# Weight reloads into any freed slot, and token changes spread over ten products, in a fused attention and two-MLP kernel

## The chip, the cores and the metric

The kernel runs as one program on one core of a Trainium2 chip. The metric is the device time of one launch in microseconds (us). Five engines work side by side: TensorE (PE, with its weight loads listed apart as PEld), VectorE (DVE), ScalarE (ACT), GpSimd (POOL) and SyncE (SP), which issues all of this kernel's DMAs. Each engine takes its own instructions in the order in which they were written; semaphores hold an instruction until what it reads has been made and what it overwrites has been read.

## The reference

```python
# attention: 4 batches, 8 heads, 576 tokens, head size 64, with a relative-position bias
attn_out = softmax(q @ k.T / 8 + bias) @ v          # -> x, 2304 tokens x 512
# first MLP, 512 -> 2048 -> 512
h = x @ w_in
x = (h - tanh(h)) @ w_out
# second MLP, 512 -> 1536 -> 512, gated
gate = 1 / (1 + exp(-(x @ w_gate)))
val = x @ w_val
out = (gate * val) @ w_out
```

All of it is in float32. The kernel splits each factor of a matrix product into a rounded part ("high", dtype fp32r) and the rest ("low") and adds three products, high by high, high by low and low by high.

## The kernel before, in words

Attention runs first, then the first MLP in 48 steps, then the second MLP. The change touches only the second MLP.

**Products and slots.** The second MLP takes its 1536 hidden features as six blocks of 256 (`fp`) and its 2304 tokens as three parts of 768 (`tau`). `SEGS` orders the work as five segments, each one token part with a run of feature blocks; a block in a segment is a *pair*, and there are 18 pairs (3, 3, 6, 3 and 3). Gate and value are made by a seven-product scheme (like Strassen's): seven combinations of the weights meet seven combinations of the tokens. A pair therefore has 14 *slots*, seven products for the gate (slots 0 to 6) and seven for the value (7 to 13). `slot2` writes one slot: it issues pending weight reloads (`feed`), writes the product (L866, six matmuls of 128x384 into one of two PSUM banks, `sum0` and `sum1`), then one piece of the output product of the pair before (`down`, L882, three matmuls of 128x512; twelve of the 14 slots have one, slots 12 and 13 have none), and then `evacuate`, which takes the bank's result out of PSUM. The product of slot s needs the bank that was used in slot s - 2, so its result must have been taken out by then. Most results are taken out by VectorE with an addition or a product (L927, L933, L937, L941, one operand in PSUM); the first of each seven, and the third of the gate, by ScalarE (L924, L931).

**Changing the tokens.** Between two segments the seven token combinations must be made anew. `src_load` brings the source, `combine` makes sums and differences on VectorE (L786 to L792), and `x_make` makes one half (`kp` 0 or 1) of one combination: a copy to fp32r for the high part, and a subtraction for the low part (both have line L797). In the kernel before, `x_next` does this in the slots 7 to 13 of a segment's last pair, both halves of one combination in each slot, as each combination is used there for the last time; the copies are on ScalarE, the subtractions on GpSimd for half 0 and on VectorE for half 1. I call the seven slots C0 to C6, and the slots that follow in the next segment C7 (its slot 0), C8, and so on. There are four such change-overs. The third combination also needs `combine(kp, 3)` (L792) behind it.

**Weights.** The nine weight tiles of a pair (seven combinations and two for the output product, 512 KB each) lie in DRAM (`wsc`) and are loaded into a ring of 13 SBUF slots in a fixed rotation: load number k goes where load number k - 13 was, and is issued once that one has been used up. The tiles of the blocks 3 to 5 are made on the way, in the first half of the second MLP: `convert` lets VectorE (L545 to L549), ScalarE (L533, L556) and GpSimd (L554, L604) work at one item in seven slots and stores the results from three staging slots.

Of the kernel before, what the change touches and what calls it, by code (L numbers as in the profile page):

```python
# [7 lines left out]
F32 = mybir.dt.float32  # L8
# [427 lines left out]
PRODUCTS = (1, 6, 2, 7, 5, 4, 3)  # L436
GROUPS2 = len(PRODUCTS)
SLOTS2 = 2 * GROUPS2
PER_FP = GROUPS2 + 2
X_SLOTS, T_SLOTS, RING_SLOTS = tuple(range(14)), (14, 15), 13  # L440
STAGE1 = (0, 1, 2, 3)
X0_AT = N1 - 4
SEGS = ((0, 0, 3), (1, 0, 3), (2, 0, NFP), (0, 3, NFP), (1, 3, NFP))
PAIRS = [(g, tau, fp, fp - lo, hi - lo) for g, (tau, lo, hi) in enumerate(SEGS) for fp in range(lo, hi)]
X0_STEPS = (X0_AT + 1, X0_AT + 2, X0_AT + 3)
# [189 lines left out]
def mlps(tc, st, xr, x0, W, xs, x2s, y2s, out, consts):  # L635
# [3 lines left out]
    V, A, G, T = nc.vector, nc.scalar, nc.gpsimd, nc.tensor  # L639
# [142 lines left out]
    def combine(kp, k):  # L782
        a, b = sx[kp], sx[2 + kp]
        if k == 0:
            tt_[kp] = W.slot(T_SLOTS[kp], (128, 2, TB)).bitcast(F32)
            V.tensor_sub(src(5, kp), a[:, TB:TP], a[:, 0:TB])  # L786
        elif k == 1:
            V.tensor_sub(src(7, kp), b[:, TB:TP], a[:, TB:TP])
        elif k == 2:
            V.tensor_sub(src(6, kp), b[:, TB:TP], src(5, kp))  # L790
        else:
            V.tensor_sub(b[:, 0:TB], b[:, 0:TB], src(6, kp))  # L792

    def x_make(j, kp, low):
        x, w = src(j, kp), W.slot(X_SLOTS[2 * PRODUCTS.index(j) + kp], (128, 2, TB))
        xw[j, kp] = w
        return (lambda: A.copy(w[:, 0], x)), (lambda: low.tensor_sub(w[:, 1], x, w[:, 0].bitcast(F32)))  # L797

    X0 = {X0_AT + 1: ([(kp, k) for kp in range(2) for k in range(3)], [(j, kp) for j in (1, 2) for kp in range(2)]),
          X0_AT + 2: ([], [(6, 0), (6, 1), (7, 0), (7, 1), (5, 0)]),  # L800
# [1 line left out]
          N1: ([], [(4, 0), (4, 1)])}  # L802

    loads = [(u, i) for u in range(len(PAIRS)) for i in range(PER_FP)]
    ring, held, issued, spent = [], {}, [0], set()

    def feed():
        while issued[0] < len(loads):
            k = issued[0]
            u, i = loads[k]  # L810
            fp = PAIRS[u][2]
            if (fp, i) not in W.stored or k >= len(ring) and (k < RING_SLOTS or loads[k - RING_SLOTS] not in spent):
                return
            w = W.slot(ring[k % RING_SLOTS])
            nc.sync.dma_start(w.bitcast(F32).rearrange("p a c -> p (a c)"), W.wsc[fp][i])
            held[loads[k]] = w
            issued[0] += 1

    freed = {W.of[k, f]: LAST[1, f // NPR] + (3 if k == "o" else 1) for k in "io" for f in range(FA, NF1)}
# [2 lines left out]
    def convert():  # L822
        while W.made <= W.n:
            highs, lows, mixes, conv = W.step()
            for f in conv[:2]:
                f()
                yield
            for f in highs + lows:
                f()
            for f in conv[2:]:  # L830
                f()
                yield
            for f in mixes:
                f()
            yield
            W.scan()
            yield
            yield
    banks, sums, posts, downs, res = [], [], {}, [], {}

    def at(s, f):
# [14 lines left out]

    def product(s):
        u, m, j = mat(s)
        w = held[u, j]
        p = banks[s % 2]  # L860
        fresh = j in (0, 1, 4)
        for kp in range(2):
            x = xw[PRODUCTS[j], kp]
            for i, (a, c) in enumerate(P3):
                o = 256 * m + 128 * kp
                T.matmul(p, w[:, a, o:o + 128], x[:, c], start=(fresh and kp == 0 and i == 0),  # L866
                         stop=(kp == 1 and i == 2), skip_group_check=True)
        if m:
            spent.add((u, j))

    def down():
        if not downs:
            return
        u, f, t, d, last = downs.pop(0)
        g, tau, fp, at_, n = PAIRS[u]
        h, l = res[u, f, t]
        w = held[u, GROUPS2 + f]
        begin = at_ == 0 and f == t
        end = at_ == n - 1 and f != t
        c = slice(128 * d, 128 * d + 128)  # L880
        for i, (x, a) in enumerate(((h, 0), (h, 1), (l, 0))):
            T.matmul(sums[3 * t + d], x[:, c], w[:, a], start=(begin and i == 0), stop=(end and i == 2))  # L882
        if last:
            spent.add((u, GROUPS2 + f))
        if end:
            return lambda: leave(g, t, d)

# [77 lines left out]
    def slot2(s):  # L965
        u, m, j = mat(s)
        g, tau, fp, p, n = PAIRS[u]
        W.tick()
        feed()
        product(s)  # L970
        left = down()
        evacuate(s)
        if left:
            at(s + 1, left)
        for f in posts.pop(s, []):
            f()
        if g + 1 < len(SEGS):
            if p == n - 3 and m == 1 and j < 4:
                src_load(SEGS[g + 1][0], j)
            if p == n - 2 and j < 3:  # L980
                combine(m, j)
            if p == n - 1 and m == 1:
                x_next(j)
        if SEGS[g][1] and p == n - 1 and m == 0 and j < 6:
            bring(tau, j)
        return g + 1 < len(SEGS) and (p == n - 2 and j < 3 or p == n - 1 and m == 1 and j == 2)

    def x_next(j):
        k = PRODUCTS[j]
        for kp in range(2):  # L990
            for f in x_make(k, kp, (G, V)[kp]):
                f()
        if k == 2:
            for kp in range(2):
                combine(kp, 3)

    def due(n, stage):
        return [m for m in range(n - 4, n) if ok(m) and n - m == LAGS[stage]]
# [1 line left out]
    s = 0  # L1000
    for n in range(N1 + 3):
        if n < N1:
            W.tick()
        if n == 2:
            acc = st.enter_context(tc.tile_pool(name="ps_a", bufs=4, space=PSUM, side="right"))
        acts = second(n - 1) if ok(n - 1) else []
        acts[2:2] = [lambda m=m: fourth(m) for m in due(n, 1)]
        vecs = [f for m in due(n, 0) for f in third(m)]
        low, mixes, conv = [], [], []
        if 2 <= n < N1 and n not in X0_STEPS and not any(ends(m) and block(m)[2] for m in due(n - 1, 2)):  # L1010
            h, low, mixes, conv = W.step()
            acts += h
        if n in X0:
            conv = [lambda p=p: combine(*p) for p in X0[n][0]]
        for f in acts:
            f()
        zip_run(vecs, conv)
        if n in X0:
            for p in X0[n][1]:
                h, l = x_make(*p, G)  # L1020
                h()
                low.append(l)
        if n == N1:
            only1.close()
            ev = st.enter_context(tc.tile_pool(name="p3e", bufs=6))
            upst.close()
            one = st.enter_context(tc.tile_pool(name="ps_w", bufs=1, space=PSUM))
            banks = [one.tile([128, 512], F32, name=f"sum{i}")[:, 0:TB] for i in range(2)]
            W.raw2 = st.enter_context(tc.tile_pool(name="wr2", bufs=2))
            ob2 = st.enter_context(tc.tile_pool(name="p2o2", bufs=2))  # L1030
            W.stages = RING[RING_SLOTS:]
            W.lag = 4
        for _ in range({N1: 2, N1 + 1: 5}.get(n, 0)):
            slot2(s)
            s += 1
        for m in due(n - 1, 2):
            if ends(m):
                sixth(m)
        if ok(n):
            for _ in first(n):  # L1040
                if n < 2:
                    yield
        for m in due(n, 2):
            fifth(m)
        for l in low + mixes:
            l()
        if n < N1:
            W.scan()
        if ok(n) and ok(n + 1):
            for ahead in range(1, 5):  # L1050
                if ok(n + ahead) and block(n + ahead - 1) != block(n + ahead):
                    for f, lead in ((x_split, 3), (x_load, 4)):
                        for kt in range(4):
                            if lead - kt // 2 == ahead:
                                f(block(n + ahead), kt)
        if ok(n - 1) and block(n - 1)[2] == 1 and ends(n - 1):
            partial(n - 1)
        if n == X0_AT:
            for kt in range(4):
                src_load(0, kt)  # L1060
        if n >= X0_AT:
            ring += [i for i in RING if freed[i] == n or n == X0_AT and freed[i] < n]
            ring[RING_SLOTS:] = []
            feed()
        yield
    b = odd.tile([128, 2, 512], F32, name="up")
    sums = [b[:, i] for i in range(2)] + [acc.tile([128, 512], F32, name="acc") for _ in range(4)]
    conv = convert()
    while s < SLOTS2 * len(PAIRS):
        full = slot2(s)  # L1070
        if s == SLOTS2 // 2:
            for _ in range(2):
                W.load()
        if s > SLOTS2 // 2 and not full:
            next(conv, None)
        s += 1
        yield
# [124 lines left out]
```

## Time and profile before

| | us |
|---|---|
| median of 3 runs | 1169.89 (1168.03 to 1171.68) |
| the profiled execution | 1171.4 |
| its span, first to last instruction | 1169.6 |
| TensorE busy in the span | 1122.9 (96%) |
| VectorE busy | 829.3 (71%) |
| ScalarE busy | 672.6 (58%) |
| GpSimd busy | 667.9 (57%) |
| mean granted TensorE clock | 0.989 |

The span is what the trace covers; the execution's own time is 1.8 us more. The second MLP begins at about 723 us with single products between steps of the first MLP, has TensorE to itself from about 739 us, and ends the span. An engine's idle time is listed with what ended it, as "idle before, releaser".

### The profile page before, as it was taken

How to read it: one execution, taken by the hardware profiler on the slowest of the kernel's cores; microseconds unless marked ns; L12 is line 12 of the kernel's file. 1: busy time of each engine (PE TensorE's matmuls, PEld its weight loads, DVE VectorE, ACT ScalarE, POOL GpSimd, SP SyncE). 2: the span in 40 equal slices, each digit the busy share in tenths (PEclk: the TensorE clock that was granted, in tenths of full speed). 3: DMA queues.
4: the chain of work that ended last, by engine and by line, in shares of the span. 5: the costliest groups of instructions: out<-in, count | busy, mean ns of one | idle time of the engine just before them, and what ended most of it. 6: DMA issues, size and time to landing. Idle time of an engine off the chain costs nothing.

```text
span 1169.6 us, 19994 instructions
## 1 busy us (share of the span) xinstructions
PE 1122.9 (96%) x6968; PEld 978.5 (84%) x6968; DVE 829.3 (71%) x1443; ACT 672.6 (58%) x1341; POOL 667.9 (57%) x602
## 2 busy tenths in 40 slices
PE   5679999999999999999999999999989999999998
PEld 2246776677679999999999999998879999989987
DVE  8878888888659889898889887556566523533523
ACT  7877878787657676677766667234244222423321
POOL 1047777778635555496858667455676543523532
PEclk9889999999999999999999999999999999999999
DMA  6754636373213333355665667876987875685563
GB/s 202 258 177 129 195 112 199 121 210 108 86 48 103 105 107 114 127 195 182 213 207 176 214 238 266 292 274 243 353 313 286 310 294 210 247 295 219 220 255 138
DMA packets 107636, 235.09 MB, mean 201 GB/s; under 512 B 12688, under 2 KB 52880, under 8 KB 107536
## 3 DMA queue, kind: packets, MB, share of 16 engines
q1 hardware_dynamic: 107536, 233.82, 57.7%
q8 instruction: 56, 0.92, 0.3%
q14 instruction: 44, 0.36, 0.1%
HBM read 172.55 MB, written 61.22 MB: 200 GB/s over the span
## 4 chain that ended last, share of the span: by engine, by line
PE 86%; DMA 3%; ACT 3%; DVE 2%; issue 2%; POOL 2%; SPq 0%; DVEq 0%; ACTq 0%; POOLq 0%
PE sum L866 20%; PE acc L727 16%; PE up L663 16%; PE acc L882 8%; PE sc L227 6%; PE pv L319 6%; PE pt L269 6%; PE up L882 4%; DMA w<-wsc 2%; PE bt L75 1%; PE pv L316 1%; ACT e L86 1%; ACT y L62 1%; DMA bsc<-e 1%; POOL w L554 1%
## 5 line engine op out<-in xcount | busy, mean ns | idle before, releaser
L866 PE MATMUL sum<-w,w 128*128 128x384 f32 x1512 | 304.2, 340 | 10.4 <-DMA w<-wsc 3.3
L866 PEld LDWEIGHTS sum<-w,w 128*128 128x128 f32 x1512 | 270.2, 188 | 35.5 <-issue 5.8
L663 PE MATMUL up<-xt,w 128*128 128x384 f32 x1152 | 208.4, 335 | 0.3 <-DVE t L697 0.3
L663 PEld LDWEIGHTS up<-xt,w 128*128 128x128 f32 x1152 | 200.1, 188 | 2.9 <-issue 2.2
L727 PE MATMUL acc<-gh,w 128*128 128x384 f32 x768 | 195.5, 335 | 0.1
L259 POOL TENSOR_SCALAR n<-n,rec 128x576 f32<-128x576 f32 x144 | 120.8, 853 | 83.4 <-ACT n L248 41.1
L554 POOL TENSOR_TENSOR w<-wu,w 128x512 fp32r<-128x512 f32 x86 | 128.4, 1504 | 64.5 <-ACT w L556 64.5
L708 POOL TENSOR_TENSOR gl<-t,gh 128x384 fp32r<-128x384 f32 x96 | 103.8, 1103 | 91.2 <-issue 51.1
L727 PEld LDWEIGHTS acc<-gh,w 128*128 128x128 f32 x768 | 138.3, 188 | 1.2 <-DVE o L746 1.1
L727 PE MATMUL acc<-gl,w 128*128 128x384 f32 x384 | 128.3, 334 | 0.0
L241 DVE CUSTOM_DVE_ANT_0 n<-sc,bias 128x576 f32<-128x576 f32 x144 | 103.7, 753 | 29.7 <-PE sc L227 25.8
L916 POOL TENSOR_TENSOR gl<-e,gh 128x384 fp32r<-128x384 f32 x54 | 58.7, 1092 | 101.7 <-ACT gh L701 101.7
L248 ACT ACTIVATE n<-n,mn 128x576 f32<-128x576 f32 x144 | 111.4, 783 | 8.7 <-DVE mn L241 8.6
L701 ACT CAST gh<-t 128x384 fp32r<-128x384 f32 x114 | 57.7, 516 | 60.4 <-POOL t L952 59.3
L692 ACT ACTIVATE z<-z,c 128x768 f32<-128x768 f32 x48 | 45.2, 941 | 78.9 <-DVE up L691 78.8
L882 PE MATMUL acc<-w,gh 128*128 128x512 f32 x288 | 90.1, 393 | 0.0
L693 DVE TENSOR_TENSOR t<-up,t 128x768 f32<-128x768 f32 x48 | 46.0, 958 | 53.4 <-ACT t L680 52.7
L269 PE MATMUL pt<-ident,n 128*128 128x128 f32 x576 | 80.4, 281 | 1.4 <-ACT at L299 1.3
L654 POOL TENSOR_TENSOR xt<-xm,xt 128x384 fp32r<-128x384 f32 x48 | 49.3, 1047 | 53.9 <-ACT xt L653 50.5
L319 PE MATMUL pv<-at,vs 128*64 128x320 f32 (+1 forms) x512 | 79.3, 421 | 0.0
L941 DVE TENSOR_TENSOR e<-sum,e 128x384 f32<-128x384 f32 x70 | 38.8, 555 | 52.0 <-PE sum L866 52.0
L269 PEld LDWEIGHTS pt<-ident,n 128*128 128x128 f32 x576 | 63.5, 141 | 12.6 <-issue 11.4
(111 smaller groups left out, 2145.5 us busy)
## 6 DMA issues: line engine op xcount, KB each, us to landing
w<-wsc SPq DMA_DIRECT2D x162, 512.0 KB, 7.4
wsc<-w SPq DMA_DIRECT2D x54, 512.0 KB, 5.6
wraw<-in_wo SPq DMA_DIRECT2D x28, 512.0 KB, 4.4
bsc<-e SPq DMA_DIRECT2D x36, 295.5 KB, 3.1
xm<-xs SPq DMA_DIRECT2D x48, 192.0 KB, 3.2
x2s<-o SPq DMA_DIRECT2D x48, 192.0 KB, 3.7
wraw<-in_wi SPq DMA_DIRECT2D x16, 512.0 KB, 4.3
xt<-x2s SPq DMA_DIRECT2D x20, 384.0 KB, 6.8
```

The costliest lines, as they stand in the source:

```text
L227: T.matmul(sc[u, t][:, hf, 0:288], q[r, 128 * s:128 * s + 128], k[r, o:o + 288], start=(i == 0), stop=(i == 2))
L241: V.tensor_tensor_reduce(n.rearrange("p (a b) -> p a b", a=2), s[:, :, 0:288], bias[t].rearrange("p (a b) -> p a b", a=2), -0.125, 3.0e38, ...
L248: A.activation(n, n, AF.Exp, bias=m, scale=-1.0, accum_out=nsum[u, t // 4][:, t % 4:t % 4 + 1])
L259: G.tensor_scalar(n, n, nrec[u, t // 4][:, t % 4:t % 4 + 1], 1.0, ALU.mult, ALU.mult)
L269: T.transpose(pt[:, i], n[:, o:o + 128], ident)
L319: T.matmul(p[0][64 * a:64 * a + 64, 0:N], v[:, c - 1, a], main[:, c - 1, a * N:a * N + N], start=False, stop=(c == 4))
L554: self.nc.gpsimd.tensor_sub(w[:, 1], x, w[:, 0].bitcast(F32))
L663: T.matmul(p[:, 0:TB], w[:, a, 128 * kt:128 * kt + 128], x[:, c], start=(kt == 0 and i == 0), stop=(kt == 3 and i == 2))
L708: G.tensor_sub(l, x[:, j], h.bitcast(F32))
L727: T.matmul(ac[blk][d][:, 0:TB], w[:, a, 128 * d:128 * d + 128], c, start=(begin and j == 0 and i == 0), stop=(end and j == NPR - 1 and i = ...
L866: T.matmul(p, w[:, a, o:o + 128], x[:, c], start=(fresh and kp == 0 and i == 0), stop=(kp == 1 and i == 2), skip_group_check=True)
L882: T.matmul(sums[3 * t + d], x[:, c], w[:, a], start=(begin and i == 0), stop=(end and i == 2))
```

## The change

Three things change, all of them in the second MLP.

1. **Reloads.** The fixed rotation is replaced by a list of free slots: a slot goes onto the list when its tile has been used for the last time, and the next load takes the slot that has been free longest. Loads are still issued in the order of their use. There are 12 slots for loads instead of 13, and four staging slots instead of three.
2. **Token changes.** Half 0 of a combination is made one slot behind its last use (C1 to C7) and half 1 four slots behind (C4 to C10). Half 1's copy is on VectorE, directly before its subtraction. `combine(kp, 3)` follows the third combination one slot later, at C4 for half 0 and C7 for half 1.
3. **Conversion.** One item takes six slots instead of seven. Conversion pauses in slots that have two or more of the new token pieces (C4 to C7); before, it paused in C2.

```diff
-X_SLOTS, T_SLOTS, RING_SLOTS = tuple(range(14)), (14, 15), 13
+X_SLOTS, T_SLOTS, RING_SLOTS = tuple(range(14)), (14, 15), 12
+X_LAGS = (1, 4)
...
-    def x_make(j, kp, low):
+    def x_make(j, kp, low, copy=A.copy):
         x, w = src(j, kp), W.slot(X_SLOTS[2 * PRODUCTS.index(j) + kp], (128, 2, TB))
         xw[j, kp] = w
-        return (lambda: A.copy(w[:, 0], x)), (lambda: low.tensor_sub(w[:, 1], x, w[:, 0].bitcast(F32)))
+        return (lambda: copy(w[:, 0], x)), (lambda: low.tensor_sub(w[:, 1], x, w[:, 0].bitcast(F32)))
...
-    ring, held, issued, spent = [], {}, [0], set()
+    free, held, issued = [], {}, [0]
+
+    def spend(key):
+        free.append(held[key][0])
 
     def feed():
-        while issued[0] < len(loads):
-            k = issued[0]
-            u, i = loads[k]
+        while issued[0] < len(loads) and free:
+            u, i = loads[issued[0]]
             fp = PAIRS[u][2]
-            if (fp, i) not in W.stored or k >= len(ring) and (k < RING_SLOTS or loads[k - RING_SLOTS] not in spent):
+            if (fp, i) not in W.stored:
                 return
-            w = W.slot(ring[k % RING_SLOTS])
+            k = free.pop(0)
+            w = W.slot(k)
             nc.sync.dma_start(w.bitcast(F32).rearrange("p a c -> p (a c)"), W.wsc[fp][i])
-            held[loads[k]] = w
+            held[u, i] = k, w
             issued[0] += 1
...
             W.scan()
             yield
-            yield
...
         if m:
-            spent.add((u, j))
+            spend((u, j))
...
-            if p == n - 1 and m == 1:
-                x_next(j)
+            if p == n - 1 and m == 1 and j == 0:
+                x_next(s)
+        for f in extra.pop(s, []):
+            f()
...
-    def x_next(j):
-        k = PRODUCTS[j]
-        for kp in range(2):
-            for f in x_make(k, kp, (G, V)[kp]):
+    extra, full = {}, set()
+
+    def x_next(s):
+        def make(j, kp):
+            for f in x_make(j, kp, (G, V)[kp], (A.copy, V.tensor_copy)[kp]):
                 f()
-        if k == 2:
-            for kp in range(2):
-                combine(kp, 3)
+        for i, j in enumerate(PRODUCTS):
+            for kp, lag in enumerate(X_LAGS):
+                if j == 2:
+                    extra.setdefault(s + i + lag + 1, []).append(lambda kp=kp: combine(kp, 3))
+                extra.setdefault(s + i + lag, []).append(lambda j=j, kp=kp: make(j, kp))
+        full.update(x for x, f in extra.items() if len(f) > 1)
```

VectorE at the last change-over, in the kernel before. `sum` is a PSUM bank, `xt` the token source, `w_12217`, `w_12235` and so on are combinations, half 1:

```order
L797 TENSOR_TENSOR w_12217<-xt,w_12217 128x384
L927 TENSOR_TENSOR e<-sum_9038,e 128x384
L797 TENSOR_TENSOR w_12235<-w_12016,w_12235 128x384
L933 TENSOR_TENSOR e<-sum_9039,e 128x384
L797 TENSOR_TENSOR w_12252<-xt,w_12252 128x384
L792 TENSOR_TENSOR xt<-xt,w_11931 128x384
L792 TENSOR_TENSOR xt<-xt,w_12016 128x384
L937 TENSOR_TENSOR t<-sum_9038,e 128x384
L797 TENSOR_TENSOR w_12274<-xt,w_12274 128x384
L941 TENSOR_TENSOR t<-sum_9039,t 128x384
```

Each slot has one piece on a bank and one subtraction (C0 to C4 are shown). The same place on VectorE in the changed kernel, from C4 to C8, whose lines are numbered some three higher:

```order
L944 TENSOR_TENSOR t<-sum_9039,t 128x384
L798 CAST w_12279<-xt 128x384
L798 TENSOR_TENSOR w_12279<-xt,w_12279 128x384
L793 TENSOR_TENSOR xt<-xt,w_11929 128x384
L944 TENSOR_TENSOR e<-sum_9038,e 128x384
L798 CAST w_12298<-w_12014 128x384
L798 TENSOR_TENSOR w_12298<-w_12014,w_12298 128x384
L944 TENSOR_TENSOR e<-sum_9039,e 128x384
L798 CAST w_12317<-xt 128x384
L798 TENSOR_TENSOR w_12317<-xt,w_12317 128x384
L793 TENSOR_TENSOR xt<-xt,w_12014 128x384
L798 CAST w_12342<-xt 128x384
```

The copy (CAST) now stands on VectorE before each subtraction, and the whole of half 1 has moved four slots down.

SyncE's weight loads of one pair, late in the second MLP, in the kernel before, with the semaphores that each waits for (PE_49 is TensorE's, DMAHW are those of the DMA queues):

```order
L815 DMA w_12068<-wsc_2_112 128x1024 [waits DMAHW7_49,PE_49]
L815 DMA w_12070<-wsc_3_113 128x1024 [waits DMAHW0_49]
L815 DMA w_12072<-wsc_4_114 128x1024 [waits DMAHW1_49]
L815 DMA w_12074<-wsc_5_115 128x1024 [waits DMAHW2_49]
L815 DMA w_12076<-wsc_6_116 128x1024 [waits DMAHW3_49]
```

Only the first has a wait for TensorE; two more loads without one follow. The same loads in the changed kernel:

```order
L819 DMA w_12031<-wsc_2_112 128x1024 [waits DMAHW7_49,PE_49]
L819 DMA w_12033<-wsc_3_113 128x1024 [waits DMAHW0_49,PE_49]
L819 DMA w_12047<-wsc_4_114 128x1024 [waits DMAHW1_49,PE_49]
L819 DMA w_12063<-wsc_5_115 128x1024 [waits DMAHW2_49,PE_49]
L819 DMA w_12076<-wsc_6_116 128x1024 [waits DMAHW3_49,PE_49]
```

Each load now has a wait for TensorE of its own, the two that follow too.

## Rows read from the trace of the kernel before

**Rows 1.** The page: the span, TensorE's busy time, VectorE's busy tenths in 40 slices.

```profile
span 1169.6 us, 19994 instructions
...
PE 1122.9 (96%) x6968; PEld 978.5 (84%) x6968; DVE 829.3 (71%) x1443; ACT 672.6 (58%) x1341; POOL 667.9 (57%) x602
...
DVE  8878888888659889898889887556566523533523
```

**Rows 2.** TensorE's waits from 738 us on: us in total, times, longest.

```profile
PE sum L866 <- DMA w<-wsc: 3.3, 3, 1.6
PE sum L866 <- DVE t L941: 3.1, 2, 1.7
```

**Rows 3.** The chain in order of time, second MLP: start, duration, engine, line, count.

```profile
768.76 3.14 PE sum L866 x18
...
845.02 3.14 PE sum L866 x18
...
919.37 3.14 PE sum L866 x18
...
1012.27 2.21 PE sum L866 x12
...
1154.92 2.10 PE sum L866 x12
```

**Rows 4.** The timeline of TensorE: start, duration, what, idle before it and releaser.

```profile
794.72 1.32 PE L866 MATMUL sum<-w,w 128*128 128x384 f32 x6 [1.40 <-DVE t L941]
...
827.20 1.28 PE L866 MATMUL sum<-w,w 128*128 128x384 f32 x6 [1.11 <-DMA w<-wsc]
...
1012.11 3.69 PE L866 MATMUL sum<-w,w 128*128 128x384 f32 x18
...
1035.69 3.30 PE L866 MATMUL sum<-w,w 128*128 128x384 f32 x18
```

**Rows 5.** The timeline of VectorE and GpSimd at the first and third change-over.

```profile
786.47 1.07 POOL L797 TENSOR_TENSOR w<-w,w 128x384 fp32r<-128x384 f32 x1 [0.21 <-ACT w L797]
...
786.59 1.23 DVE L547 TENSOR_SCALAR wu<-wu 128x512 f32<-128x512 f32 x1
...
1009.51 1.84 DVE L792 TENSOR_TENSOR xt<-xt,w 128x384 f32<-128x384 f32 x2
...
1009.91 1.02 POOL L797 TENSOR_TENSOR w<-xt,w 128x384 fp32r<-128x384 f32 x1 [0.74 <-ACT w L797]
```

**Rows 6.** VectorE's groups, shapes apart: count, busy us, mean ns, idle before.

```profile
L549 DVE SCALAR_TENSOR_TENSOR wu<-wraw,wu 128x512 int32<-128x512 int32 x68 | 62.9, 925 | 0.1
L545 DVE SCALAR_TENSOR_TENSOR wu<-wraw,wu 128x512 int32<-128x512 int32 x68 | 61.8, 909 | 0.5
L547 DVE TENSOR_SCALAR wu<-wu 128x512 f32<-128x512 f32 x68 | 59.9, 881 | 3.0 <-ACT wu L533 3.0
...
L941 DVE TENSOR_TENSOR e<-sum,e 128x384 f32<-128x384 f32 x70 | 38.8, 555 | 52.0 <-PE sum L866 52.0
L548 DVE TENSOR_SCALAR wu<-wu 128x512 int32<-128x512 int32 x68 | 38.5, 565 | 0.1
...
L797 DVE TENSOR_TENSOR w<-xt,w 128x384 fp32r<-128x384 f32 x20 | 18.8, 941 | 13.0 <-ACT w L797 13.0
...
L792 DVE TENSOR_TENSOR xt<-xt,w 128x384 f32<-128x384 f32 x10 | 7.6, 793 | 0.0
```

**Rows 7.** Lines L547 and L797: duration in ns, min/median/max, first and last start.

```profile
L547 DVE TENSOR_SCALAR wu<-wu x68: 417/920/1316, 45.5 to 924.9; 128x512 f32<-128x512 f32 x68
...
L797 DVE TENSOR_TENSOR w<-xt,w x20: 541/906/1281, 785.6 to 1088.0; 128x384 fp32r<-128x384 f32 x20
```

**Rows 8.** Line L815, the weight loads: from issue to landing.

```profile
DMA to landing us min/median/max: 3.6/7.4/11.5
```

**Rows 9.** Windows of 1 us: busy PE, PEld, DVE, ACT, POOL; granted clock, DMA share, GB/s.

```profile
797.00:798.00 1.00, 0.55 (x2) 0.58 (x3) 1.00 (x2) 1.00 (x3) 1.00 (x2) 0.50 1.05 418
...
800.00:801.00 1.00, 1.00 (x6) 0.89 (x5) 0.00 (x0) 0.69 (x2) 1.00 (x2) 0.87 1.00 406
```

More of the change, by code (lines that the diff above doesn't have):

```diff
@@ L858, in product @@
         u, m, j = mat(s)
-        w = held[u, j]
+        w = held[u, j][1]
         p = banks[s % 2]
@@ L876, in down @@
         h, l = res[u, f, t]
-        w = held[u, GROUPS2 + f]
+        w = held[u, GROUPS2 + f][1]
         begin = at_ == 0 and f == t
@@ L883, in down @@
         if last:
-            spent.add((u, GROUPS2 + f))
+            spend((u, GROUPS2 + f))
         if end:
@@ L981, in slot2 @@
                 combine(m, j)
-            if p == n - 1 and m == 1:
-                x_next(j)
+            if p == n - 1 and m == 1 and j == 0:
+                x_next(s)
+        for f in extra.pop(s, []):
+            f()
         if SEGS[g][1] and p == n - 1 and m == 0 and j < 6:
             bring(tau, j)
-        return g + 1 < len(SEGS) and (p == n - 2 and j < 3 or p == n - 1 and m == 1 and j == 2)
-    def x_next(j):
-        k = PRODUCTS[j]
-        for kp in range(2):
-            for f in x_make(k, kp, (G, V)[kp]):
-                f()
-        if k == 2:
-            for kp in range(2):
-                combine(kp, 3)
+        return g + 1 < len(SEGS) and p == n - 2 and j < 3 or s in full
+    extra, full = {}, set()
+    def x_next(s):
+        def make(j, kp):
+            for f in x_make(j, kp, (G, V)[kp], (A.copy, V.tensor_copy)[kp]):
+                f()
+        for i, j in enumerate(PRODUCTS):
[4 more added lines that the diff above has]
+        full.update(x for x, f in extra.items() if len(f) > 1)
     def due(n, stage):
@@ L1061, in mlps @@
         if n >= X0_AT:
-            ring += [i for i in RING if freed[i] == n or n == X0_AT and freed[i] < n]
-            ring[RING_SLOTS:] = []
+            free += [i for i in RING[:RING_SLOTS] if freed[i] == n or n == X0_AT and freed[i] < n]
             feed()
@@ L1069, in mlps @@
     while s < SLOTS2 * len(PAIRS):
-        full = slot2(s)
+        crowded = slot2(s)
         if s == SLOTS2 // 2:
@@ L1073, in mlps @@
                 W.load()
-        if s > SLOTS2 // 2 and not full:
+        if s > SLOTS2 // 2 and not crowded:
             next(conv, None)
```

## The prediction

> **What bounds the kernel now.** I read the page first, then TensorE's waits, the chain in order of time, the timelines around each gap, and last the prices. TensorE is busy for 1122.9 of 1169.6 us [rows 1], so nothing in this kernel can win much beyond TensorE's gaps. From 738 us on, where the change acts, they end on a weight load (3.3 us in three waits) and on VectorE's L941, which frees a PSUM bank (3.1 us in two) [rows 2].
>
> How much is there to win? The chain shows it better than the waits, for it also holds matmuls that were stretched. Its groups of three products start in slot 12 of a pair [rows 3]. From 919.37 to 1012.27, in four pairs without a gap, a pair takes 23.2 us. A product takes 3.14 / 3 = 1.05, so an output piece takes (23.2 - 14 x 1.05) / 12 = 0.71. Against 23.2 per pair:
>
> - 768.76 to 845.02, three pairs with the first change-over: 76.26 - 69.6 = 6.7 too long. Of this 1.1 is a wait for weights [rows 4], so 5.6 is the change-over. In it the granted clock stood at 0.50, which is 1.2 of 2.4 GHz, from 797 to 800.9, after TensorE had twice waited 1.4 [rows 4, 9]; it worked from 797.45 on, so that cost 3.4 x 0.5 = 1.7.
> - 845.02 to 919.37, with the second: 74.35 - 69.6 = 4.75.
> - 1012.27 to 1154.92, six pairs with the third and fourth: 142.65 - 139.2 = 3.45. The other two weight waits are 2.2 of it, so 1.25 is left for two change-overs, 0.6 each. It shows in the products C5 to C7, which take 3.69 at the third change-over and 3.30 in the next pair, without any idle row [rows 4].
>
> So 11.6 us hang on the change-overs and 3.3 on the loads. If all went, 14.9 of 1171.4 would.
>
> **Reloads.** With 13 slots in rotation, a pair's third load waits for the output tile that the pair before uses up in its slot 11. It is issued in slot 12 and needed in slot 2: slots 12, 13, 0 and 1, or 2 x 1.05 + 2 x 1.76 = 5.6 us, while a load lands in 3.6 to 11.5, median 7.4 [rows 8]. In the changed order the shortest lead is from slot 8 to slot 1: four slots of 1.76, two of 1.05, one of 1.76, together 10.9 us; and the seven loads no longer leave at one moment. I take all 3.3 us as won. At worst nothing is, if the largest landing of 11.5 meets the lead of 10.9 often. The added waits on SyncE's queue hold up only what stands behind them there, mainly stores of finished rows and raw weights, by a slot or so; nothing on TensorE waits for those at present [rows 2]. One load slot fewer is in these leads already. A fourth staging slot and the faster conversion shift work that TensorE does not wait for outside the change-overs; VectorE, at 5 to 8 tenths there [rows 1], covers conversion at 7/6 of its density. I take nothing for them; without that cover some tenths per slot would show.
>
> **Change-overs: VectorE's bill.** The gap arises since VectorE takes its work in order: what stands ahead of L941 delays the bank. So I add up what VectorE has in seven slots and set it against TensorE's seven slots, 7 x 1.05 + 5 x 0.71 = 10.9 us (C5 and C6 have no output piece, before and after). Means are from [rows 6].
>
> Before, C0 to C6: six results from the banks x 0.555, seven subtractions L797 x 0.941, two L792 x 0.793: 3.33 + 6.59 + 1.59 = 11.5, which is 0.6 above 10.9. Measured: 0.6. With the four conversion pieces of one item (0.881 + 0.565 + 0.925 + 0.909 = 3.3) it is 3.9 above; measured 5.6 - 1.7 = 3.9 and 4.75. The bill prices all four within a us, so I use it for the changed kernel.
>
> After, C4 to C10: five results (C7's and C9's go to ScalarE) 2.78, seven subtractions 6.59, two L792 1.59: 11.0, before a single copy. Seven copies on VectorE are added. Conversion pauses in C4 to C7; at the first change-over three pieces fall into C8 to C10 (L548, L549, L545: 2.4), at the second one (L545, 0.9), at the others none. What half 1 leaves behind in C0 to C3 is no help: VectorE is idle in part there, but an in-order queue can't draw work forward.
>
> The price of the copy, a 128x384 cast from SBUF to SBUF, is not in the trace. Its nearest row is L547, one SBUF source, 128x512: 0.417 alone, up to 1.316 [rows 7]. Scaled to 384 that is an estimate of 0.31 alone. Why the rows spread: at 786.59 an L547 took 1.23 and ended 0.28 behind GpSimd's subtraction, which ran from 786.47 to 787.54; at 1009.51 two L792 took 1.84 together, and ended 0.42 behind GpSimd's subtraction of 1009.91 to 1010.93 [rows 5]. VectorE's work on SBUF operands and GpSimd's exclude each other, and each operation of VectorE lets one of GpSimd past. The Trainium skill states this too (SBUF — State Buffer, "SBUF: two separate sides"): the shared port pair is an exclusive lock, held for a whole instruction, against GpSimd by a VectorE operation with two SBUF inputs or in a two-port mode; the trace agrees with the 1.23 us above. By that rule the copies are held up and the sum is the one below; without it they would cost 0.31 to 0.54, the first rival's sum.
>
> GpSimd is full just there: in C4 to C8 it has four subtractions of half 0, three products with the gate and three of the low parts, ten operations of about 1.02 [rows 5], 10.2 us against the 7.4 of these five slots. So I add to the copy the wait that L797 shows in the same place, 0.941 - 0.541 = 0.40 [rows 6, 7]: 0.71, and 5.0 for seven. The bounds are 0.31 (2.2) and 1.316 (9.2).
>
> - Third and fourth: 11.0 + 5.0 - 10.9 = 5.1 each, 10.2.
> - Second: 5.1 + 0.9 = 6.0.
> - First: 5.1 + 2.4 = 7.5, and 1.7 for the clock as before, 9.2.
>
> Sum 25.4, against 11.6: 13.8 more. Less 3.3 of loads: +10.5 us. The profiled execution took 1171.4 and would take 1181.9. It lies 1.5 above the median of the runs, 1169.9, so I forecast 1180.4. The gain that the edit does bring, ScalarE with seven copies fewer and VectorE no longer waiting for them (13.0 us of idle time before L797 [rows 6]), is mostly at the first pieces of a change-over, where no bank is late.
>
> With the copy at 0.31, each change-over is 2.8 shorter: 14.2, or 12.5 if the clock then holds, which less 3.3 gives -0.7 to -2.4 and 1167.5 to 1169.2. At 1.316 each is 4.2 longer: +27, near 1197.
>
> **The rivals.**
>
> *The copies run beside GpSimd* (0.31 to 0.54 each). For it: no one-source fp32r copy of VectorE is in the trace. Against it: L547 has one source as well and is held up. Time: 1167.5 to, at 0.54, 1169.9 + 25.4 - 4 x 1.2 - 11.6 - 3.3 = 1175.6; its middle is about 1171, no change.
>
> *The spreading works.* Half 1's copies fall into time in which VectorE waited for ScalarE, as its 13.0 us of waits would allow [rows 6], and cost the path nothing. Then the four are 0.1, 0.1, 1.0 and 2.5, together 3.7: 1169.9 - 7.9 - 3.3 = 1158.7, faster. Against it: the bill is over 10.9 before the first copy.
>
> *Worse: the clock.* A wait of some 3 us falls in each change-over, and the clock falls in all four as it did in the first: three times 1.7 more, 1185.5. It decides from the point where the gaps exceed those of 1.4 that the first had. Against it: that a gap brings the clock down rests on one case here.
>
> *The reloads don't help*, as the loads share the DMA engines at full load in the change-overs (share 1.05 and 1.00 [rows 9]): 3.3 more, 1183.7.
>
> **How the numbers follow.** Forecast 45%; clock in all four 8%; loads without gain 5%; copies beside GpSimd 22%; spreading works 20%. A measurement of this kernel tells about 0.3% from no change, 1166.4 to 1173.4. Faster: the spreading rival and a little of the copies' lower end, 22%. Slower: the first three, with what the copies' upper end adds and less the forecast's low tail, 58%. The rest, 20%, is the same. The forecast's own range is 1174 to 1190. To hold 8 in 10 the range must reach to the spreading rival: 1159 to 1190, with about 1 in 10 left out at either end.
>
> **What would show it.** Right: VectorE's L798 casts far above 0.31 (0.7 in the mean) where GpSimd is busy; TensorE waiting for VectorE in the products C6 to C10 of all four change-overs, the third and fourth too, which had 0.6 each; no waits for w<-wsc left. Wrong: casts near 0.31 to 0.4, or C4 to C10 without a gap at the third change-over. The pair's distance in the chain at the third change-over decides: 23.8 if I am wrong, 28.3 if I am right.

## The result, and the profile after

| | us |
|---|---|
| before, median of 6 runs | 1171.24 (1168.03 to 1173.13) |
| changed, median of 6 runs | 1184.54 (1182.49 to 1186.55) |
| ratio changed to before | 1.0116, 95% interval 1.0097 to 1.0135 |
| profiled execution, before and changed | 1171.4 and 1183.05 |
| span, before and changed | 1169.6 and 1181.1 |

The change made the kernel slower by 1.2%, some 13 us. The prediction had said 10.5 more. TensorE's largest waits after 738 us, in the changed kernel, in us in total, times and longest:

```profile
PE sum L869 <- DVE e L930: 7.7, 4, 2.3
PE sum L869 <- issue: 5.4, 3, 1.9
PE sum L869 <- DMA w<-wsc: 2.0, 1, 2.0
PE sum L869 <- DVE t L940: 1.9, 1, 1.9
```

The waits for weights went from 3.3 in three to 2.0 in one [rows 2]; the loads land sooner than before [rows 8], from issue to landing:

```profile
DMA to landing us min/median/max: 3.2/6.2/9.3
```

What grew is the rest: L930 and L940 are VectorE's work on the banks, held back by what stands ahead of it. The chain in order of time gives each change-over its size:

```profile
767.05 3.14 PE sum L869 x18
...
847.53 3.14 PE sum L869 x18
...
900.01 3.15 PE sum L869 x18
...
992.81 3.14 PE sum L869 x18
...
1043.97 3.14 PE sum L869 x18
...
1067.37 3.14 PE sum L869 x18
...
1120.07 3.14 PE sum L869 x18
...
1166.47 2.10 PE sum L869 x12
```

All start in slot 12 of a pair, and a pair still takes 23.2 where nothing waits (from 900.01 to 992.81, four pairs, 92.80). Three pairs with the first change-over took 80.48, that is 10.9 too many, 2.0 of them the weight wait; two pairs with the second 52.48, 6.1 too many; with the third 51.16, 4.8; with the fourth 52.70, 6.3. Before, they were 5.6, 4.75 and twice 0.6 [rows 3, 4]. So 14.5 us were lost in change-overs and 1.3 won on weights. The chain from 767.05 to 1166.47 is 13.3 longer than the one of before. The spans differ by less, 11.5, as this chain began 1.7 earlier (767.05 against 768.76 [rows 3]); in the nine traces of the case that point lies between 764.6 and 768.8, so the 1.7 is not shown to be the change's doing.

VectorE at the third change-over, C4 to C10, in the timeline (start, duration, line, what):

```profile
1015.83 0.92 DVE L798 CAST w<-xt 128x384 fp32r<-128x384 f32 x1
1016.78 1.25 DVE L798 TENSOR_TENSOR w<-xt,w 128x384 fp32r<-128x384 f32 x1
1017.96 1.34 DVE L793 TENSOR_TENSOR xt<-xt,w 128x384 f32<-128x384 f32 x1
1019.22 0.55 DVE L944 TENSOR_TENSOR e<-sum,e 128x384 f32<-128x384 f32 x1
1019.69 0.34 DVE L798 CAST w<-w 128x384 fp32r<-128x384 f32 x1
1020.07 1.25 DVE L798 TENSOR_TENSOR w<-w,w 128x384 fp32r<-128x384 f32 x1
...
1024.91 1.17 DVE L798 CAST w<-xt 128x384 fp32r<-128x384 f32 x1
1026.11 1.23 DVE L798 TENSOR_TENSOR w<-xt,w 128x384 fp32r<-128x384 f32 x1
1027.27 0.55 DVE L930 TENSOR_TENSOR e<-sum,e 128x384 f32<-128x384 f32 x1
```

No row has an idle time, so VectorE is the bound here. Each L944 or L930 frees a bank, and stands behind a cast, a subtraction and sometimes an L793. TensorE's two gaps end on two of these:

```profile
1019.87 1.28 PE L869 MATMUL sum<-w,w 128*128 128x384 f32 x6 [1.75 <-issue]
...
1027.86 1.32 PE L869 MATMUL sum<-w,w 128*128 128x384 f32 x6 [2.26 <-DVE e L930]
```

The first is C7's product, which ends its wait just behind the L944 of 1019.22; the view names no releaser for it. The second is C10's, just behind the L930 of 1027.27. Why VectorE is slow shows on GpSimd:

```profile
1019.85 1.06 POOL L955 TENSOR_TENSOR e<-e 128x384 f32<-128x384 f32 x1 [0.96 <-DVE e L944]
...
1024.54 1.32 POOL L798 TENSOR_TENSOR w<-xt,w 128x384 fp32r<-128x384 f32 x1
```

The cast of 1019.69 began while GpSimd was idle and took 0.34. The subtraction behind it lasted until 1021.32, 0.41 behind the end of GpSimd's L955. The cast of 1024.91 lasted 1.17, until 0.22 behind the end of GpSimd's subtraction at 1025.86. So a cast from SBUF to SBUF waits for GpSimd too. The Trainium skill states of the shared port pair (SBUF — State Buffer, "SBUF: two separate sides") that a VectorE operation in a two-port mode and one of GpSimd block each other for a whole instruction. The trace agrees, 1.17 against 0.34, if the cast runs in such a mode, which no row tells. VectorE's groups over all change-overs (busy us, mean ns, idle before):

```profile
L798 DVE TENSOR_TENSOR w<-xt,w 128x384 fp32r<-128x384 f32 x20 | 19.4, 971 | 0.7
L798 DVE CAST w<-xt 128x384 fp32r<-128x384 f32 x20 | 13.6, 680 | 0.0
L793 DVE TENSOR_TENSOR xt<-xt,w 128x384 f32<-128x384 f32 x10 | 12.4, 1238 | 0.1
...
L798 DVE TENSOR_TENSOR w<-w,w 128x384 fp32r<-128x384 f32 x8 | 8.2, 1027 | 0.3
...
L798 DVE CAST w<-w 128x384 fp32r<-128x384 f32 x8 | 4.9, 615 | 0.0
```

A cast took 18.5 / 28 = 0.66 in the mean, twice its 0.34 alone. VectorE's 13.0 us of waiting for ScalarE before L797 [rows 6] are gone (0.7 left), and nothing was won by it. They go by the later place of half 1 alone: 0.7 is left as well where ScalarE makes the copies in that place (experiment 1).

### The profile page after: what moved, and what is told of

It reads as the page before. It is cut to its first block, busy times and chain, and to the rows that moved or that the text cites. A ratio compares the mean times of both kernels' runs of the same rounds, so it can differ in the third digit from the quotient of the medians.

```text
span 1181.1 us, 20081 instructions
## 1 busy us (share of the span) xinstructions
PE 1124.1 (95%) x6968; PEld 981.5 (83%) x6968; DVE 849.7 (72%) x1471; ACT 659.8 (56%) x1313; POOL 669.7 (57%) x602
## 4 chain that ended last, share of the span: by engine, by line
PE 85%; DVE 6%; DMA 3%; ACT 3%; issue 2%; POOL 1%; SPq 0%; DVEq 0%; ACTq 0%; POOLq 0%
PE sum L869 20%; PE acc L728 16%; PE up L664 16%; PE acc L885 7%; PE sc L227 6%; PE pv L319 6%; PE pt L269 6%; PE up L885 4%; DVE w L798 3%; PE bt L75 1%; PE pv L316 1%; ACT y L62 1%; DMA bsc<-e 1%; DVE xt L793 1%; ACT e L86 1%
## 5 line engine op out<-in xcount | busy, mean ns | idle before, releaser
L869 PEld LDWEIGHTS sum<-w,w 128*128 128x128 f32 x1512 | 273.4, 190 | 44.1 <-DVE e L930 9.5
L241 DVE CUSTOM_DVE_ANT_0 n<-sc,bias 128x576 f32<-128x576 f32 x144 | 103.7, 753 | 33.2 <-PE sc L227 23.7
L944 DVE TENSOR_TENSOR e<-sum,e 128x384 f32<-128x384 f32 x70 | 38.8, 555 | 50.7 <-PE sum L869 50.3
```

The costliest lines, as they stand in the source:

```text
L241: V.tensor_tensor_reduce(n.rearrange("p (a b) -> p a b", a=2), s[:, :, 0:288], bias[t].rearrange("p (a b) -> p a b", a=2), -0.125, 3.0e38, ...
```

## The experiments

The theory was VectorE's bill: seven copies too many in an in-order queue that also waits for GpSimd. Its rivals were the new place of half 1 in C4 to C10, VectorE's load without GpSimd's part in it, and the reloads.

**1. Copies on ScalarE.** The changed kernel with one edit:

```diff
-            for f in x_make(j, kp, (G, V)[kp], (A.copy, V.tensor_copy)[kp]):
+            for f in x_make(j, kp, (G, V)[kp], (A.copy, A.copy)[kp]):
```

> The changed kernel with half 1's copies on ScalarE again; slots, reloads and conversion stay as changed. Theory (VectorE's bill with seven copies of 0.66): the bill of C4 to C10 falls to about 11 us against TensorE's 10.9, so the four change-overs cost about 4 to 6 us together where the changed kernel has 26; with its single weight wait of 2.0 that is about 1163 us, ratio 0.990 to 0.995 to the kernel before. Rival (the place, not the copies: half 1 now lies on the two short slots C5 and C6 and four slots nearer to its use): the gaps before C7 and C10 stay, 1180 or more.

Measured: 1165.3 us, ratio to the kernel before 0.9952 (0.9936 to 0.9968). The chain:

```profile
842.00 3.14 PE sum L869 x18
889.18 3.17 PE sum L869 x18
...
982.00 3.14 PE sum L869 x18
1029.31 3.14 PE sum L869 x18
1052.51 3.14 PE sum L869 x18
1099.85 3.14 PE sum L869 x18
```

The second, third and fourth change-over (889.18 - 842.00 - 46.4, and so on) are down to 0.8, 0.9 and 0.9. In the first stretch 5.9 are left beside the weight wait of 1.9; 1.7 of them go to a fall of the clock behind that wait (0.50 from 831 to 834), where six matmuls took 2.12 (832.09) in place of 1.22. So the first change-over kept 4.2, and the four cost 6.8 and not 4 to 6: in the first the conversion's three pieces come in C8 to C10, and TensorE waited 1.55 and 0.97 for VectorE in the products that follow. The place of half 1 is thus not at fault by itself; seven casts on VectorE in place of seven copies on ScalarE cost 1.0116 / 0.9952, some 19 us. About five of them come by way of the clock: the changed kernel's trace has four stretches at half clock in the change-overs (below), this one has none there and one behind its weight wait.

**2. Reloads alone.** The kernel before with the free list, 12 load slots and four staging slots; token changes and seven-slot conversion as they were.

```diff
-X_SLOTS, T_SLOTS, RING_SLOTS = tuple(range(14)), (14, 15), 13
+X_SLOTS, T_SLOTS, RING_SLOTS = tuple(range(14)), (14, 15), 12
...
-            if (fp, i) not in W.stored or k >= len(ring) and (k < RING_SLOTS or loads[k - RING_SLOTS] not in spent):
+            if (fp, i) not in W.stored:
                 return
-            w = W.slot(ring[k % RING_SLOTS])
+            k = free.pop(0)
+            w = W.slot(k)
...
```

> The kernel before with the free list, twelve load and four staging slots alone; token changes and conversion as before. Theory: the weight waits fall from 3.3 to 0 to 2 us, the change-overs stay at about 11.6: 1168 to 1170 us, ratio 0.997 to 0.999. Rival (the reloads cost: each load waits for TensorE and holds up SyncE's queue): weight waits above 3.3 or gaps elsewhere, ratio above 1.002.

Measured: 1168.17 us, ratio 0.9975 (0.9964 to 0.9986). No wait for w<-wsc is left on TensorE, as the prediction had it. The time fell by 2.9 us (1.6 to 4.2 by the interval), which fits the 3.3 of waits. Its change-overs did not stay at 11.6: in its trace they took 13.3, since the clock fell in the second, which cost 2.0 more than in the kernel before (last section).

**3. Casts in the old slots.** The kernel before with half 1's copies on VectorE in C0 to C6:

```diff
...
-            for f in x_make(k, kp, (G, V)[kp]):
+            for f in x_make(k, kp, (G, V)[kp], (A.copy, V.tensor_copy)[kp]):
```

> The kernel before with one edit: half 1's copies on VectorE, in the old slots C0 to C6. Theory (copies add to a bill that is full): 7 x 0.66 = 4.6 per change-over, less what VectorE no longer waits for ScalarE at the first pieces (2.5): 2 to 5 each, ratio 1.007 to 1.016. Rival (copies fill time in which VectorE waited for ScalarE, and only the new slots are at fault): ratio 0.998 to 1.002.

Measured: 1182.96 us, ratio 1.0103 (1.0084 to 1.0123). The casts alone, without any other part of the change, bring a loss of 12 us, nearly as large as the whole change's. That is less than their 19 in the new slots (experiment 1), so the new place, which costs nothing without the casts, or what else goes with it there, makes them dearer. A cast took 0.60 in the mean here:

```profile
L797 DVE CAST w<-xt 128x384 fp32r<-128x384 f32 x20 | 11.4, 569 | 4.8 <-PE sum L866 4.8
...
L797 DVE CAST w<-w 128x384 fp32r<-128x384 f32 x8 | 5.4, 680 | 0.0
```

**4. GpSimd relieved.** The changed kernel, where half 0's low part is made by a second copy of ScalarE and not by GpSimd's subtraction. VectorE has the same instructions.

```diff
-            for f in x_make(j, kp, (G, V)[kp], (A.copy, V.tensor_copy)[kp]):
-                f()
+            h, l = x_make(j, kp, (G, V)[kp], (A.copy, V.tensor_copy)[kp])
+            h()
+            if kp:
+                l()
+            else:
+                A.copy(xw[j, kp][:, 1], src(j, kp))
```

> The changed kernel, but half 0's low part is a second copy by ScalarE in place of GpSimd's subtraction; the low part of half 0 is thus not subtracted. It takes 28 operations of about 1.02 us off GpSimd and leaves VectorE's work as it is. Theory (the copies and subtractions of VectorE wait for GpSimd's, one for one): the copies fall from 0.66 to 0.40 to 0.50 in the mean, the subtractions from 0.97 to 0.75, and each change-over from some 6 to 2 to 3 us: about 1170 us, ratio 0.995 to 1.003. Rival (VectorE simply has too many instructions, GpSimd does not matter): durations and gaps unchanged, ratio 1.009 to 1.013.

Measured: 1169.86 us, ratio 0.9993 (0.9978 to 1.0007), so some 14 us come back by an edit that takes nothing off VectorE. The groups:

```profile
L798 DVE TENSOR_TENSOR w<-xt,w 128x384 fp32r<-128x384 f32 x20 | 16.7, 836 | 0.7
...
L798 DVE TENSOR_TENSOR w<-w,w 128x384 fp32r<-128x384 f32 x8 | 9.7, 1211 | 0.3
L793 DVE TENSOR_TENSOR xt<-xt,w 128x384 f32<-128x384 f32 x10 | 9.0, 902 | 0.1
L798 DVE CAST w<-xt 128x384 fp32r<-128x384 f32 x20 | 8.4, 420 | 0.0
...
L798 DVE CAST w<-w 128x384 fp32r<-128x384 f32 x8 | 4.5, 561 | 0.0
```

The casts fell from 0.66 to 12.9 / 28 = 0.46 and L793 from 1.24 to 0.90; the subtractions hardly (0.99 to 0.94, where 0.75 was expected), as they still meet GpSimd's other work. In the third change-over two pairs took 48.31 (chain, 989.03 to 1037.34), 1.9 too many in place of 4.8. The five groups took 48.3 us in place of 58.5, which is 10.2 less; three falls of the clock fewer in the change-overs (one in place of four) give some 5 more. Against that the weight waits were 3.2, 1.2 more than in the changed kernel, and the clock fell behind them. That VectorE's operations wait for GpSimd's is shown with this.

**5. Copies on ScalarE, conversion at seven slots.** The first experiment's kernel with the `yield` put back that the change took out of `convert`:

```diff
             W.scan()
             yield
+            yield
```

> The first experiment's kernel (half 1's copies on ScalarE, new slots, new reloads) with the conversion back at seven slots per item. Theory (the weight wait of 1.9 us that is left near 830 us comes from the faster conversion, whose two stores come just ahead of the pair's last product load on SyncE's queue and on full DMA engines): no weight wait, as with the reloads alone, and change-overs no longer than the first experiment's: 1160 to 1164 us, ratio 0.990 to 0.994. Rival (the wait comes from the later token pieces, or the faster conversion pays elsewhere): the wait of about 2 us stays, ratio 0.994 to 0.998.

Measured: 1164.05 us, ratio 0.9943 (0.9922 to 0.9963), the fastest kernel of the case, though not apart from the first experiment's. My theory of the weight wait fell: it is still there.

```profile
827.29 1.28 PE L870 MATMUL sum<-w,w 128*128 128x384 f32 x6 [2.13 <-DMA w<-wsc]
...
876.70 1.31 PE L870 MATMUL sum<-w,w 128*128 128x384 f32 x6 [1.56 <-DVE t L941]
879.68 1.33 PE L870 MATMUL sum<-w,w 128*128 128x384 f32 x6 [0.96 <-DVE t L945]
```

The two gaps of the conversion (1.56 and 0.96) have moved from the first change-over to the second: at seven slots it is there that an item's pieces come in C8 to C10.

**6. Reloads, conversion at six slots.** The second experiment's kernel with that `yield` taken out:

```diff
             W.scan()
             yield
-            yield
```

> The reloads alone (second experiment) with the conversion at six slots per item, token changes as before. Theory of the weight wait (faster conversion): a wait of about 2 us on w<-wsc comes back near 830 us and nothing else changes, ratio 0.998 to 1.001 where the reloads alone had 0.9975. Rival: no weight wait, ratio 0.996 to 0.998.

Measured: 1167.21 us, ratio 0.9974 (0.996 to 0.9988). A weight wait of 1.90 came back near 830 us, as the theory had it, but the time did not rise: its second change-over cost 3.2 where the second experiment's cost 6.6, as the conversion's pieces fell elsewhere and the clock held. So the six slots alone and the new token slots alone each bring the weight wait; neither is its only cause. And the faster conversion shows no worth by itself (0.9974 against 0.9975).

**7. Stores four slots later.** The first experiment's kernel with one edit:

```diff
-            W.lag = 4
+            W.lag = 8
```

> The first experiment's kernel with stores and raw loads of the conversion issued eight slots behind their making instead of four. It asks for the weight wait of 1.9 us near 830 us, which neither seven slots per item nor the old token slots took away when each was combined with the other edit. Theory (three kinds of transfers meet there: four source loads, two stores and the pair's reloads, so that the reload issued in slot 12 leaves late on SyncE's queue and lands late): with the two stores out of the way the wait falls below 0.5 us, ratio 0.992 to 0.995. Rival (the reload itself lands late, since the DMA engines are full of reloads and source loads): the wait stays at 1.5 to 2.2, ratio 0.994 to 0.997.

Measured: 1165.33 us, ratio 0.9958 (0.9938 to 0.9978). The wait stayed, 2.14 at 831.83, as the rival had it. But the edit was no clean test of the theory: it moved another store (817.60) and two raw loads (821.32 and 822.94) to the place that the two stores had left. The 6 us window ahead of the wait (last three columns: granted clock, DMA share, GB/s):

```profile
824.00:830.00 6.00, 5.68 (x29) 4.87 (x27) 3.92 (x7) 2.32 (x5) 4.51 (x5) 1.00 1.05 405
```

The DMA engines are full. But with the reloads alone they were full there too, at 417 GB/s, and TensorE did not wait. What differs is when the reload leaves, and the trace of the changed kernel shows it. There TensorE waits for the seventh load of a pair, which SyncE issued at 828.16. First what SyncE waited for before it issued this load, then the time to landing of this load and of the token load issued at 820.07:

```profile
836.75 1.29 PE L869 MATMUL sum<-w,w 128*128 128x384 f32 x6 [1.99 <-DMA w<-wsc]
```

```profile
SPq L819 <- DMA xt<-x2s: 0.9, 1, 0.9
...
w<-wsc SPq DMA_DIRECT2D x1, 512.0 KB, 8.5
...
xt<-x2s SPq DMA_DIRECT2D x1, 384.0 KB, 8.0
```

SyncE held the load until that token load, the eighth transfer before it, had landed at 828.09. So it is with every DMA that SyncE issued from 823 to 830.1: each left within 0.1 us of the landing of the eighth one before it. With some 8 us to a landing, the load of 828.16 left 6.6 us ahead of its use, where the same load of most pairs leaves 13 ahead, and landed 2 us too late. In the trace of the reloads alone it left 7.8 ahead and landed in 7.6, so that a wait was missed by less than 0.2 us. The last 2 us are thus a late issue behind eight transfers under way. Which of these would have to move was not tried.

## Why the prediction was right

**The reloads.** Forecast 3.3 won, with a bound of nothing. Alone they took away all 3.3 of waits (experiment 2); in the changed kernel 1.3, since one wait of 2.0 remains, which is nearer to the rival's nothing than to my 3.3. The bound had the wrong reason, a landing of 11.5 that outlasts a lead of 10.9: no landing took more than 9.3, but a lead was 6.6. I had let the waits on SyncE's queue hold up "mainly stores", by a slot or so; they held up a reload by five slots (experiment 7).

**The copy's price.** Forecast 0.71: 0.31 alone and 0.40 of waiting for GpSimd. Measured 0.66: 0.34 alone and 0.32 of waiting. Taking the wait from L797, which stood in the same place, was what hit; L547's smallest row alone would have given 0.31, and with it a forecast of no change.

**The change-overs.** Forecast 9.2, 6.0, 5.1 and 5.1, together 25.4; measured 8.9, 6.1, 4.8 and 6.3, together 26.1. TensorE waited before C7 and C10 of all four, as forecast, and before C12 of the first. The pair of the third took 51.16 - 23.2 = 28.0, where I had set 28.3 against 23.8. That the sum comes out so closely is in part luck. The clock fell four times, twice in the first change-over and once in the second and the fourth, and I had counted one fall. The two of the first, and the second's from its first whole microsecond to its end:

```profile
796.00:797.00 1.00, 1.00 (x4) 0.80 (x3) 0.96 (x3) 1.00 (x3) 1.00 (x2) 0.50 1.01 414
...
809.00:810.00 1.00, 1.00 (x4) 0.90 (x4) 1.00 (x3) 0.08 (x1) 0.00 (x0) 0.50 0.00 0
...
884.00:885.00 1.00, 1.00 (x4) 0.83 (x3) 0.97 (x4) 0.00 (x0) 0.00 (x0) 0.50 0.00 0
...
887.00:888.00 1.00, 1.00 (x6) 0.87 (x5) 0.56 (x2) 0.53 (x1) 0.00 (x0) 0.82 0.14 57
```

In the second change-over it stood at 0.50 from 884 to 887.4 while TensorE worked, which costs 1.7 by an estimate; the two of the first were as long, and the fourth change-over took 1.5 more than the third. Together that is 6.6, where I had 1.7. Without the clock the four are 5.5, 4.4, 4.8 and 4.8, together 19.5, where the bill had 23.7. The conversion pieces that I had added, 2.4 in the first and 0.9 in the second, made these 0.7 dearer and no dearer than the third. So the bill was 4 us too high and the clock 5 too low, and the two errors hid each other. L793 was dearer than its old mean, 1.24 in place of 0.79; of the bill that these prices give, 2.78 + 6.9 + 2.5 + 4.6 = 16.8 against 10.9, about 1 us did not reach TensorE in the third change-over. Why is not shown; I take it that a bank is free to be late by a little.

**The rivals.** That the copies run beside GpSimd is out: 0.66, and 0.46 where GpSimd has less (experiment 4). That the spreading works is out for the copies on VectorE, but right for the slots: with the copies left on ScalarE the same slots cost 0.8 to 0.9 in three of four change-overs (experiment 1). I had not separated the two. That the clock falls in all four came nearly true, in the cost too: 4.9 more than I had counted, where that rival had 5.1. My words against it, that a gap brings the clock down rests on one case, missed a row on the other side: in the kernel before, the second change-over's gaps of 1.67 and 1.69 brought no fall (last section).

**The total.** +10.5 was forecast; the medians differ by 13.3 and the profiled executions by 11.65. The chain misses 2.7 of its 13.2: the weight wait of 2.0 that remained and 0.7 more in the change-overs. The profiled executions differ by less only because the later chain began 1.7 earlier.

## What to carry to other kernels

Before work is moved to an engine with idle time, add up what that engine has in the few microseconds where it must also free a buffer, and set that sum beside the time of the engine that waits; a busy share of five tenths over the stage [rows 1] says nothing of a stretch of 11 us. An operation of VectorE on SBUF next to a busy GpSimd is priced by the rows of its neighbours there, not by its shortest row. And where a change has several parts, one of them may carry the whole loss: here the reloads, the slots and ScalarE's copies together are 0.5% faster than the kernel before.

## What the runs showed of the hardware that was not expected

The third and the fourth change-over of the changed kernel had the same two gaps, 1.75 and 2.26 us, and the granted clock fell behind the second gap only in the fourth. The product behind it in the fourth:

```profile
1102.42 2.29 PE L869 MATMUL sum<-w,w 128*128 128x384 f32 x6 [2.26 <-DVE e L930]
```

Six matmuls took 2.29 at the fourth and 1.32 behind the same gap at the third (the row of 1027.86), where the granted clock was 1.00 from 1028 to 1030. In the second change-over the kernel before had gaps of 1.67 and 1.69 and experiment 2 gaps of 1.66 and 1.69. Behind the second gap, in the kernel before and then in experiment 2:

```profile
874.25 1.28 PE L866 MATMUL sum<-w,w 128*128 128x384 f32 x6 [1.69 <-issue]
```

```profile
871.83 2.26 PE L870 MATMUL sum<-w,w 128*128 128x384 f32 x6 [1.69 <-issue]
```

The first ran at full clock, the second at half. So whether a gap of this size costs another 1.5 to 2.0 us is not settled by the gap alone.

VectorE and GpSimd take turns, one for one, when both have SBUF work waiting; that a long row of VectorE's gets no two turns together I had read from one pair of rows only [rows 5]. It holds: in the rows of the third change-over each subtraction of VectorE that met GpSimd took 1.23 to 1.25 and GpSimd's operations between them 1.06 to 1.33, in place of 0.56 and 1.02 alone. From 1022.45 to 1027.27 VectorE got through four such operations, casts and subtractions alike, one in 1.2 us: a chain of short operations on VectorE goes at GpSimd's pace.
